# A transformer block on one core: where the MLP phase puts its weight parts, its turned features and its boundary additions

## The chip, the cores and the metric

The kernel runs on one core of a Trainium2 chip. The metric is the device time of one execution in microseconds. A core has five engines, each with a stream of instructions of its own: TensorE (PE in the profile, its weight loads PEld) multiplies matrices into the accumulator memory PSUM, VectorE (DVE), ScalarE (ACT) and GpSimd (POOL) work element by element, and SyncE (SP) issues most DMAs. Engines wait for each other by semaphores only.

## The reference, cut to what matters

One transformer block for 2048 tokens of width D = 640, with a modulation vector made from `c`. First comes an attention half with a linear kernel, which gives A1. The second half is the one in which the change lies:

```python
x = x + ga * A                                   # A1 holds ga * A
h = layernorm(x) * (1 + cb) + sb
r = relu(h @ w1 + b1); r = r * r                 # w1: 640 x 1728
x = x + gb * (r @ w2 + b2)                       # w2: 1728 x 640
```

All is float32. TensorE gets float32 precision from the faster format float32r by splitting each matrix into a high part and a low part and adding three products (high by high, high by low, low by high). So each operand needs a copy that rounds (ScalarE, the high part) and a subtraction (VectorE, the low part).

## The kernel before, in words

The attention half ends about 401 us after the start. The MLP phase, from there to the end, works on blocks of 256 tokens, j = 0 to 7 (`NB` = 8), each held as two tiles i = 0, 1 of 128 tokens. The 1728 columns of w1 are cut into 14 pieces f (13 of 128, the last of 64), taken in pairs n = 0 to 6 (`NP` = 7). So a block is seven steps n, and a step has two half steps, one for each f.

In each half step `up(j, f)` makes the hidden columns (15 matmuls into PSUM tile `up`), ScalarE applies bias and relu (line 1162, `ft<-up`) and VectorE squares (line 1163). After the second half step `split_a` makes high and low part of the squares (`ra`; ScalarE lines 1186 and 1192, VectorE line 88). One step later the products with w2 run as `down(0)` and `down(1)`, one behind each `up`: their stationary operand is `ra`. Blocks 0 and 1 are plain (`PLAIN` = 2): four regions "2", "3", "4", "x" of the result are summed directly. In later blocks most pairs use a scheme with seven products instead of eight, for which sums of hidden columns (`rs`, lines 1177 and 1202) and sums of weights (`ring_a`, `ring_b`, `ring_c`, fetched from DRAM by GpSimd's queue, line 1272, into four buffers) are needed. The accumulators are PSUM banks. Regions 3 and x share one.

Beside these matmuls, the other engines prepare what comes next, and the order in which they do it is written out by hand in the loop of lines 1430 to 1516, for all engines but SyncE. SyncE's DMAs are ordered by the planner, and run as far ahead as their buffers allow.

- **Weight parts.** A part is one of the 28 pieces of w1 and w2. `prep(k)` (line 1377) makes k of them: k copies (`p_hi`, ScalarE line 938), k subtractions (`p_lo`, VectorE line 88, `w<-rw`), and k loads of raw rows for later parts (`p_load`, SyncE lines 928 and 931, `rw<-in_w`). Nine parts are done before the MLP phase. The other 19 are made in block 0: `PREPS` (line 1389) says how many at each of the two calls in a step. `down` and `up` of block 0 need each part a step or more later.
- **LayerNorm of the next block.** `layer(j + 1, at)` (line 1411), with at = 2n or 2n + 1, does what the tables `LN_AT` give for that half step: `load_x1` loads A1 into `xm` and x into two rows `xx`; `add_x` adds them (VectorE line 997) and stores the sum in DRAM (line 998); `ln_pieces` gives six ScalarE pieces, two sums (line 1396) and two squares (line 1401), which write their unused full-size output into the rows `xx`, and two scalings (line 1408), with small work on GpSimd; `t2` turns the normalised tokens: TensorE transposes (line 359, `tb`), ScalarE scales into a buffer `hf` (line 370), ScalarE rounds it (line 371, `h<-hfb`), VectorE subtracts (line 88, `h<-hfb`). `hf` is one buffer of 256 columns in the pool `p3`.
- **The end of a block.** At n = 0 of the next block `first_combos` adds some regions, and `end` adds region by region into the rows `y` (VectorE line 1327; for blocks 0 and 1 line 1330 multiplies by the gate instead), `gate` multiplies by gb, `finish` adds the residual and stores. The residual rows `xr` are loaded from the stored sums (`residual`, line 1317), and `add_bias` (line 1319) adds gb * b2 to them.

Rows of 640 columns come from sets of buffers: `s1` has five, `s2` two. A row asked for from a set waits until the row that last used the slot has been read for the last time. `row("s1", ...)` is used for raw weights, residuals, and the rows `xx` from block 3 on. The w1 weights of f = 13 live in one row of s1 to the end. `s2` holds `y`, the rows `xx` of blocks 1 and 2, and the raw rows of the two parts f = 13 (64 wide).

Of the kernel before, what the change touches and what calls it, by code (L numbers as in the profile page):

```python
# [51 lines left out]
def kernel(  # L52
# [64 lines left out]
    def row(tag, name):  # L117
        return (pc if tag in ("s3", "s4") else mem).tile([P, D], F32, tag=tag, name=name, bufs=BUFS[tag])
# [793 lines left out]
    def prep_load(k, f, w):  # L912
        n = FS[f]
        W = W1 if k == "1" else W2
        if k == "1":
            w = w.rearrange("p s (k n) -> p s k n", k=NC)
        W[f] = w
        i = preps.index((k, f))
        if EARLY_ROWS <= i < EARLY_ROWS + 4:
            if i % 2 == EARLY_ROWS % 2:  # L920
                RAWT.append(tok2(f"w{W_AT[(-19, -16)[len(RAWT)]]}", f"rawt{i}"))
            raw = RAWT[-1][:, (i - EARLY_ROWS) % 2]
        else:
            raw = row("s2" if n < P else "s1", f"rw{k}_{f}")
        if k == "1":
            raw = raw.rearrange("p (k n) -> p k n", k=NC)
        if k == "1":
            nc.sync.dma_start(raw, w1[f * P : (f + 1) * P].rearrange("p (k n) -> p k n", k=NC))
        else:
            for r in range(P // n):  # L930
                nc.sync.dma_start(raw[r * n : r * n + n], w2[f * P : f * P + n])
        RAW[k, f] = raw
# [67 lines left out]
    def t2(j, *ds):  # L1000
        if 0 in ds:
            H2[j] = ht(f"h2_{j}", j, (0, 96))
        if j == 0:
            t_unit(XM[j], cols_b, H2[j], ds[0], f"b{j}", bank(f"tb{j}_{ds[0]}"))
            return
        p = tp(f"tb{j}_{ds[0]}")
        for k, d in enumerate(ds):
            t_in(XM[j], d, p[:, 256 * k : 256 * k + 256])
        for k, d in enumerate(ds):
            hf = p3.tile([P, 256], F32, tag="hf", name=f"hfb{j}_{d}")  # L1010
            t_out(cols_b, H2[j], d, f"b{j}", p[:, 256 * k : 256 * k + 256], hf)

    NB = NT // 2
    places += [new(f"w{w}") for w in W_AT[-23:-19] + W_AT[-18:-16] + W_AT[-15:]] + [new(tag) for tag in ("k", "k", "q0", "q1")]
# [304 lines left out]
    def add_bias(j, i):  # L1319
        add(XR[j, i], XR[j, i], bb)  # L1320
# [56 lines left out]
    def prep(n):  # L1377
        p_hi(n)
        p_lo(n)
        p_load(n)  # L1380
# [5 lines left out]
    LN_AT1 = {"load": 3, "add": (5, 5), "ln": (5, 6, 6, 7, 8, 8), 9: (0, 1), 11: (2, 3), 12: (4,)}  # L1386
    LN_AT2 = {"load": 4, "add": (6, 6), "ln": (7, 7, 8, 8, 9, 9), 10: (0, 1), 11: (2, 3), 12: (4,)}
    LN_AT = {"load": 0, "add": (3, 4), "ln": (4, 5, 6, 6, 7, 7), 8: (0, 1), 10: (2, 3), 12: (4,)}
    PREPS = iter([0, 4] * 5 + [0, 1])

    def ln_pieces(xt, nm, spare):
        sm = small([P, 2], "sm", f"sm{nm}")
# [15 lines left out]
            nc.scalar.activation(xt[:, i], xt[:, i], AF.Identity, bias=nb[:, i : i + 1], scale=sq[:, i : i + 1])  # L1408
            yield

    def layer(j, at):
        todo = {1: LN_AT0, PLAIN: LN_AT1, PLAIN + 1: LN_AT2}.get(j, LN_AT)
        if j == NB:
            return
        if at in todo:
            t2(j, *todo[at])
        if todo["load"] == at:
            load_x1(j)
        for i in range(2):
            if todo["add"][i] == at:  # L1420
                add_x(j, i)
        for i in range(6):
            if todo["ln"][i] == at:
                if i == 0:
                    LN2[j] = ln_pieces(XM[j], f"b{j}", XX[j])
                next(LN2[j])
# [3 lines left out]
    for j in range(NB):  # L1430
        for n in range(NP):
            down = lambda k: prev and (down_plain if plain(*prev) else down_pair)(*prev, k)
            twice = not plain(j, n)
            m = NP * j + n - NP - 1
            done = j - 1 if j and prev else None
            up(j, 2 * n)
            if prev and not plain(*prev):
                split_s(*prev)
            down(0)
            if j < PLAIN:  # L1440
                layer(j + 1, 2 * n)
            if 0 < m < NP - 2:
                t_split(m - 1)
            if m == -1:
                t_load(0)
            if (j, n) == (PLAIN, 0):
                t_fetch(4)
            if j >= PLAIN:
                layer(j + 1, 2 * n)
            prep(next(PREPS, 0))  # L1450
            if n == 0 and j:
                if j - 1 >= PLAIN:
                    first_combos(j - 1)
                else:
                    Y[j - 1] = [row("s2", f"y{j - 1}_{i}") for i in range(2)]
                for r, i, c in (("2", 0, L), ("3", 0, R)):
                    end(j - 1, r, i, c)
            if n == 1 and j:
                gate(j - 1, 0)
                if j != PLAIN:  # L1460
                    finish(j - 1, j < PLAIN)
            if n == 1 and j == PLAIN:
                finish(j - 1, 0)
            if n == 2 and j == PLAIN:
                t_sums(NP - 2)
            if n == (2 if j > PLAIN else 1) and j:
                gate(j - 1, 1)
            if n == (5, 5, 4, 3)[min(j, 3)]:
                residual(j)
            for i in range(2):  # L1470
                if n == 6 and j == 0 or n == 5 and j >= PLAIN and i == 0:
                    add_bias(j, i)
            if j == NB - 1 and n == 1:
                for k in range(NP - LAST, NP - 1):
                    plain_load(k)
            if j == NB - 1 and n == 3:
                for k in range(NP - LAST, NP - 1):
                    plain_split(k)
            if j == NB - 1 and n == NP - 2:
                for i in range(2):  # L1480
                    by_gate(Y[j][i], Y[j][i], slice(0, D))
            if j == NB - 1 and n == NP - 1:
                split_a(j, n, (0,))
                for i in range(2):
                    add(Y[j][i], Y[j][i], XR[j, i])
            up(j, 2 * n + 1)
            if j >= PLAIN and n == 0:
                down(1)
            split_a(j, n, (0, 1) if (j, n) != (NB - 1, NP - 1) else (1,))
            if twice:  # L1490
                sums(j, n)
            if j < PLAIN or n:
                down(1)
            if m == NP + 1:
                t_split(NP - 2)
            prep(next(PREPS, 0))
            if n == 0 and j:
                end(j - 1, "4", 1, L)
                end(j - 1, "x", 1, R)
            if n == (2 if j > PLAIN else 1 if j == PLAIN else 0) and j:  # L1500
                finish(j - 1, j >= PLAIN)
            layer(j + 1, 2 * n + 1)
            if 0 <= m < NP - 2:
                t_sums(m)
            if m == NP - 2:
                t_split(m - 1)
            if 0 < m + 1 < NP - 1:
                t_load(m + 1)
            if m == NP - 1:
                for i in range(2):  # L1510
                    add_bias(j - 1, i)
            if j >= PLAIN and n == 5:
                add_bias(j, 1)
            if j == NB - 1 and n == NP - LAST:
                first_combos(j)
            prev = j, n
# [60 lines left out]
```

## Time and profile before

| | |
|---|---|
| median of 3 runs | 789.05 us (789.01 to 789.47) |
| the profiled execution | 788.85 us |
| span of the profile, first to last instruction | 787.1 us |
| mean granted TensorE clock | 0.998 |
| TensorE busy | 775.0 us, 98% of the span |
| VectorE, ScalarE, GpSimd busy | 583.9, 441.3, 124.3 us |
| share of the DMA engines in use, 401 to 494 / 494 to 547 / 547 to 779 us | about 0.57 / 0.88 / 0.63 |

In the lists of waits a row says which engine and line waited for which, with the total, the number and the longest in microseconds. In a timeline a row gives start, length, engine, line, operation, what is written from what, the shape and how many were merged; a bracket holds the idle time of that engine before the row and what ended it. Line 78 is a helper that issues all matmuls and line 88 one for all low parts, so that the tiles' names tell them apart.

### The profile page before, as it was taken

Reading aid. Unit: us, or ns where it says so; the run is one execution under the profiler, and the core shown is the slowest. Engines: PE = TensorE matmul, PEld = TensorE weight load, DVE = VectorE, ACT = ScalarE, POOL = GpSimd, SP = SyncE. Lnnn points to the kernel's source line nnn. Section 1 sums busy time; section 2 is a strip of 40 time slices with the busy share of each in tenths; the row PEclk is TensorE's granted clock in tenths of the full one; section 3 lists DMA queues with packets and bytes.
Section 4 is the critical chain, followed back from the end, with each engine's and each line's share of the span. In section 5 each row is a group of like instructions: output and inputs, shape, how many; then the busy total and the mean of one; then the engine's idle time right before and its main releaser. Section 6 shows DMA issues by size and latency. Waiting matters only on the chain.

```text
span 787.1 us, 15302 instructions
## 1 busy us (share of the span) xinstructions
PE 775.0 (98%) x5989; PEld 745.6 (95%) x5989; DVE 583.9 (74%) x1059; ACT 441.3 (56%) x988; POOL 124.3 (16%) x253
## 2 busy tenths in 40 slices
PE   9999999999999999999999999999999999999997
PEld 8899999999999889998999999999999999999997
DVE  6599899998788699986256666775757567585756
ACT  5766675475752365656766636455454645536331
POOL 3001101001000232320000001131131313213110
PEclk9999999999999999999999999999999999999999
DMA  9714244432120254222266365897675858657450
GB/s 336 281 59 139 83 152 156 134 113 89 68 102 1 83 169 168 84 100 85 101 194 209 101 208 207 289 319 229 177 221 167 266 149 264 204 169 211 117 168 34
DMA packets 50551, 126.03 MB, mean 160 GB/s; under 512 B 5991, under 2 KB 6759, under 8 KB 50479
## 3 DMA queue, kind: packets, MB, share of 16 engines
q1 hardware_dynamic: 33144, 83.99, 31.1%
q0 software_dynamic: 14752, 35.76, 16.3%
q10 hardware_dynamic: 2583, 5.30, 1.7%
q8 instruction: 47, 0.77, 0.4%
q14 instruction: 25, 0.20, 0.1%
HBM read 95.05 MB, written 29.88 MB: 159 GB/s over the span
## 4 chain that ended last, share of the span: by engine, by line
PE 82%; DVE 5%; DMA 5%; ACT 4%; issue 3%; POOL 1%; POOLq 0%; SPq 0%; ACTq 0%; DVEq 0%
PE up L78 19%; PE acc L78 14%; PE pwo L78 10%; PE pk L78 9%; PE pq L78 8%; PE pv L78 8%; PE acc3x L78 4%; PE kvp L440 3%; PE te L850 2%; DMA ring_b<-td_b 1%; PE numa L78 1%; DMA wm<-in_w_ss 1%; PE tb L359 1%; PE numc L78 1%; PE numb L78 1%
## 5 line engine op out<-in xcount | busy, mean ns | idle before, releaser
L78 PE MATMUL up<-h,w 128*128 128x256 f32 x1640 | 207.1, 278 | 0.4 <-ACT ft L1162 0.4
L78 PEld LDWEIGHTS up<-h,w 128*128 128x128 f32 x1640 | 196.3, 188 | 0.8 <-ACT ft L1162 0.6
L1162 ACT ACTIVATE ft<-up,b_t 128x256 f32<-128x256 f32 x104 | 48.8, 469 | 104.0 <-PE up L78 103.5
L78 PE MATMUL acc<-w,ra 128*128 128x384 f32 x452 | 100.1, 338 | 1.0 <-ACT ra L1186 1.0
L78 PE MATMUL pwo<-wo,ot 128*128 128x256 f32 (+3 forms) x512 | 81.1, 311 | 0.0
L1163 DVE TENSOR_TENSOR ft<-ft 128x256 f32<-128x256 f32 x104 | 44.0, 423 | 48.9 <-ACT ft L1162 47.2
L78 PE MATMUL pk<-wk,hT 128*128 128x384 f32 (+1 forms) x480 | 77.7, 312 | 0.2 <-ACT hT L371 0.2
L78 PEld LDWEIGHTS pwo<-wo,ot 128*128 128x128 f32 (+1 forms) x512 | 74.9, 188 | 2.7 <-issue 2.7
L78 PEld LDWEIGHTS acc<-w,ra 128*128 128x128 f32 x452 | 72.6, 188 | 4.1 <-DVE ra L88 2.8
L78 PE MATMUL pv<-wv,hT 128*128 128x384 f32 (+1 forms) x480 | 76.0, 309 | 0.0
L78 PE MATMUL pq<-wq,hT 128*128 128x384 f32 (+1 forms) x480 | 74.5, 311 | 0.4 <-ACT k L416 0.4
L78 PEld LDWEIGHTS pk<-wk,hT 128*128 128x128 f32 x480 | 71.8, 188 | 2.0 <-ACT hT L371 0.8
L78 PEld LDWEIGHTS pq<-wq,hT 128*128 128x128 f32 x480 | 70.6, 188 | 1.4 <-ACT k L416 0.9
L78 PEld LDWEIGHTS pv<-wv,hT 128*128 128x128 f32 x480 | 70.7, 188 | 0.4
L88 DVE TENSOR_TENSOR ra<-ft,ra 128x384 fp32r<-128x384 f32 (+2 forms) x86 | 36.8, 448 | 34.2 <-ACT ra L1186 21.5
L1186 ACT ACTIVATE ra<-ft 128x384 fp32r<-128x384 f32 x48 | 25.2, 525 | 32.6 <-DVE ft L1163 25.2
L88 DVE TENSOR_TENSOR h<-hfb,h 128x256 fp32r<-128x256 f32 x40 | 17.0, 425 | 35.1 <-ACT h L371 35.1
L78 PE MATMUL acc3x<-w,ra 128*128 128x256 f32 x248 | 43.0, 281 | 0.0
L78 PEld LDWEIGHTS acc3x<-w,ra 128*128 128x128 f32 x248 | 39.5, 188 | 1.6 <-DVE y L1327 1.4
L1272 POOL DMA_DIRECT2D ring_a<-td_a x34 | 18.3, 538 | 128.1 <-PE acc L78 107.4
L1177 DVE TENSOR_TENSOR ft<-ft 128x128 f32<-128x128 f32 x136 | 33.3, 286 | 1.2
L370 ACT ACTIVATE hfb<-tb,cols_b 128x256 f32<-128x256 f32 x40 | 22.5, 562 | 18.9 <-PE tb L359 11.3
(251 smaller groups left out, 1407.7 us busy)
## 6 DMA issues: line engine op xcount, KB each, us to landing
ring_c<-td_c POOLq DMA_DIRECT2D x34, 384.0 KB, 4.5
ring_a<-td_a POOLq DMA_DIRECT2D x34, 384.0 KB, 4.1
ring_b<-td_b POOLq DMA_DIRECT2D x34, 256.0 KB, 4.0
esp<-eq SPq DMA_DIRECT2D x12, 640.0 KB, 2.9
el<-esp SPq DMA_DIRECT2D x12, 640.0 KB, 3.9
rw<-in_w SPq DMA_DIRECT2D x23, 320.0 KB, 4.5
wm<-in_w_mod SPq DMA_DIRECT2D x20, 320.0 KB, 4.3
xb<-in_x SPq DMA_DIRECT2D x8, 640.0 KB, 4.0
```

The source lines that it names most:

```text
L78: nc.tensor.matmul(o, a, b, start=first and i == 0, stop=last and i == len(terms) - 1, skip_group_check=skip,)
L88: (eng or nc.vector).tensor_tensor(out_lo, full, hi.bitcast(F32), op=ALU.subtract)
L359: nc.tensor.transpose(p[:, i * P : (i + 1) * P], xn[:, i, d * P : (d + 1) * P], ident)
L370: nc.scalar.activation(hf, p[:, :256], AF.Identity, bias=cols[:, d : d + 1], scale=cols[:, 5 + d : 6 + d])
L440: nc.tensor.matmul(kvp[g // 4][64 * c : 64 * c + 64, a : a + 2 * n].rearrange("p (s n) -> p s n", s=2), v[:, u], e[:, :, o : o + n], start ...
L850: nc.tensor.transpose(p[:m, a : a + P], EU[2 * j + i][:, b : b + m], ident)
L1162: nc.scalar.activation(r, p, AF.Relu, bias=b1_t[:, f : f + 1])
L1163: nc.vector.tensor_tensor(r, r, r, op=ALU.mult)
L1177: nc.vector.tensor_tensor(t[:, o], t[:, a], t[:, b], op=op)
L1186: nc.scalar.activation(a[:, 0, :3], t[:, :3], AF.Copy)
L1272: nc.gpsimd.dma_start(RING[j, n, r], TD[n][r].bitcast(F32R))
```

## The change

Six edits, all in the MLP phase:

1. The raw rows of the parts f = 13 are taken from s1, like all others, not from s2.
2. `t2` has no buffer `hf` of its own: it uses the first 256 columns of the two rows `xx` in turn, by d % 2. The rows stay in use until the last unit is turned (at = 12).
3. `PREPS`: before, no part in the first half step and four in the second, for five steps, and one at the end. After, two and two for three steps, two and one for two steps, and one at n = 5.
4. In the first half steps of block 0 `layer` is split: turning, loading and adding go ahead of the weight parts, the LayerNorm pieces behind them.
5. In blocks 2 to 7 the bias additions of both tiles stand at n = 5 ahead of `layer`. Before, the first stood behind it and the second at the end of the second half step.
6. At the boundary of two blocks region 3 is ended before region 2.

```diff
@@ -921,7 +921,7 @@ prep_load
-            raw = row("s2" if n < P else "s1", f"rw{k}_{f}")
+            raw = row("s1", f"rw{k}_{f}")
@@ -1007,8 +1007,7 @@ t2
         for k, d in enumerate(ds):
-            hf = p3.tile([P, 256], F32, tag="hf", name=f"hfb{j}_{d}")
-            t_out(cols_b, H2[j], d, f"b{j}", p[:, 256 * k : 256 * k + 256], hf)
+            t_out(cols_b, H2[j], d, f"b{j}", p[:, 256 * k : 256 * k + 256], XX[j][d % 2][:, :256])
@@ -1386,7 +1385,7 @@
-    PREPS = iter([0, 4] * 5 + [0, 1])
+    PREPS = iter([2, 2] * 3 + [2, 1] * 2 + [1])
@@ -1408,17 +1407,20 @@
-    def layer(j, at):
+    def layer(j, at, part=None):
         todo = {1: LN_AT0, PLAIN: LN_AT1, PLAIN + 1: LN_AT2}.get(j, LN_AT)
         if j == NB:
             return
-        if at in todo:
-            t2(j, *todo[at])
-        if todo["load"] == at:
-            load_x1(j)
-        for i in range(2):
-            if todo["add"][i] == at:
-                add_x(j, i)
+        if part != 1:
+            if at in todo:
+                t2(j, *todo[at])
+            if todo["load"] == at:
+                load_x1(j)
+            for i in range(2):
+                if todo["add"][i] == at:
+                    add_x(j, i)
+        if part == 0:
+            return
         for i in range(6):
             if todo["ln"][i] == at:
                 if i == 0:
@@ -1438,7 +1440,7 @@
             if j < PLAIN:
-                layer(j + 1, 2 * n)
+                layer(j + 1, 2 * n, None if j else 0)
@@ -1446,14 +1448,19 @@
             if j >= PLAIN:
+                if n == 5:
+                    for i in range(2):
+                        add_bias(j, i)
                 layer(j + 1, 2 * n)
             prep(next(PREPS, 0))
+            if j == 0:
+                layer(j + 1, 2 * n, 1)
             if n == 0 and j:
...
-                for r, i, c in (("2", 0, L), ("3", 0, R)):
+                for r, i, c in (("3", 0, R), ("2", 0, L)):
                     end(j - 1, r, i, c)
@@ -1468,7 +1475,7 @@
             for i in range(2):
-                if n == 6 and j == 0 or n == 5 and j >= PLAIN and i == 0:
+                if n == 6 and j == 0:
                     add_bias(j, i)
@@ -1509,8 +1516,6 @@
-            if j >= PLAIN and n == 5:
-                add_bias(j, 1)
             if j == NB - 1 and n == NP - LAST:
                 first_combos(j)
```

## The prediction

> **What bounds the kernel now.** I read the page first, then the waits of the weight loads on TensorE over the MLP phase (400 to 788 us), then the timelines around each wait. First the page, then those waits (columns: total us, times, longest).
>
> ```profile
> span 787.1 us, 15302 instructions
> ...
> PE 775.0 (98%) x5989; PEld 745.6 (95%) x5989; DVE 583.9 (74%) x1059; ACT 441.3 (56%) x988; POOL 124.3 (16%) x253
> ```
>
> ```profile
> PEld acc L78 <- DVE ra L88: 2.8, 10, 0.3
> PEld acc L78 <- DMA ring_b<-td_b: 1.8, 1, 1.8
> PEld acc3x L78 <- DVE y L1327: 1.4, 5, 0.3
> PEld acc L78 <- ACT ra L1186: 1.2, 1, 1.2
> PEld up L78 <- ACT ft L1162: 0.6, 1, 0.6
> PEld tb L359 <- ACT hfb L370: 0.4, 1, 0.4
> PEld acc L78 <- DVE rs L88: 0.3, 1, 0.3
> ```
>
> TensorE is the bound, and the change neither adds nor removes a matmul. So it can gain at most these eight or nine microseconds, and can lose only by new waits. The question is which of these rows each edit reaches. The profiled execution took 788.85 us for a span of 787.1 (1.75 lie around it), 0.20 under the median of 789.05; my sum is made from 788.85, and the 0.20 is added at the end.
>
> **Part 1: weight parts two per half step (block 0).** A weight part is one ScalarE copy, one VectorE subtraction and one load. Before, four come together in each second half step. TensorE, then ScalarE, VectorE and SyncE at that place:
>
> ```profile
> 413.29 1.03 PE L78 MATMUL acc<-w,ra 128*128 128x384 f32 x3
> ...
> 418.80 1.86 PE L78 MATMUL up<-h,w 128*128 128x256 f32 x15
> ...
> 422.58 1.86 PE L78 MATMUL up<-h,w 128*128 128x256 f32 x15
> ...
> 429.42 1.86 PE L78 MATMUL up<-h,w 128*128 128x256 f32 x15
> ...
> 432.84 2.03 PE L78 MATMUL up<-h,w 128*128 128x256 f32 x15
> 435.83 1.03 PE L78 MATMUL acc<-w,ra 128*128 128x384 f32 x3 [0.96 <-ACT ra L1186]
> ...
> 437.95 0.60 PE L359 MATMUL tb<-ident,xm 128*128 128x128 f32 x4
> ```
>
> ```profile
> 402.84 0.47 ACT L1162 ACTIVATE ft<-up,b_t 128x256 f32<-128x256 f32 x1 [0.79 <-PE up L78]
> ...
> 406.14 2.61 ACT L938 ACTIVATE w<-rw 128x640 fp32r<-128x640 f32 x4
> ...
> 411.02 0.74 ACT L1396 ACTIVATE xx<-xm 128x640 f32<-128x640 f32 x1 [1.92 <-DVE xm L997]
> ...
> 430.43 2.00 ACT L938 ACTIVATE w<-rw 128x640 fp32r<-128x640 f32 x3 [3.08 <-DMA rw<-in_w]
> 432.33 0.45 ACT L1162 ACTIVATE ft<-up,b_t 128x256 f32<-128x256 f32 x1
> ```
>
> ```profile
> 405.05 0.43 DVE L1163 TENSOR_TENSOR ft<-ft 128x256 f32<-128x256 f32 x1 [1.27 <-ACT ft L1162]
> ...
> 406.89 3.03 DVE L88 TENSOR_TENSOR w<-rw,w 128x640 fp32r<-128x640 f32 x4
> ```
>
> ```profile
> 406.86 0.33 SPq L993 DMA_DIRECT2D xx<-in_x  x1
> ...
> 424.35 0.33 SPq L928 DMA_DIRECT2D rw<-in_w  x1
> ```
>
> Undisturbed, a half step of block 0 takes 432.84 - 429.42 = 3.42 us. From 418.80 to 422.58 it is 3.78, so 0.36 is lost; from 432.84 to 437.95 it is 5.11, so 1.69 is lost. The first kind has a chain: four subtractions (3.03) hold VectorE, the addition of x waits behind them, the LayerNorm piece waits for that with ScalarE idle (1.92), the next activation stands behind the piece, and ra is late. With two parts ahead of the piece and the addition of x ahead of both, that chain is shorter by about two subtractions, 2 x 0.74 (a step, (3.03 - 0.82)/3 with an assumed 0.82 for the last). Gain 0.36 at 420.5. The group at 413.29 has the same length as the one at 435.83, 1.03, and is a twin of this wait (0.36). I give it nothing: there the first newly loaded part may meet its own load. Its bounds are +0.36, if that load goes out at once, and -0.1, if it goes out behind the x row at 406.86 and lands 4.9 us (the median below) after about 407.3.
>
> The 1.69 goes as a whole. The load at 424.35 took a row of the two-buffer set s2, and had to wait until LayerNorm had finished with the x row in it; ScalarE then sat 3.08 us in front of three parts, with the activation at 432.33 behind them. With all raw rows in s1 and the loads spread out, that row's place is free when an earlier subtraction ends, a half step before. One slot of s1 is kept for good by the last W1 weights, so four remain; each part is still loaded at least two half steps (6.8 us) before its copy.
>
> The price: at n = 0 there were no parts ahead of the second activation, now there are two. Their copies take (2.61 - 0.72)/3 = 0.63 each from 403.3 on and end by 404.6, in time for that activation. Their subtractions start at about 404.0 and hold VectorE for 0.74 + 0.74, so the square that began at 405.05 begins at about 405.5. TensorE waits for its result at 406.09 already (one of the ten waits on ra). Loss 0.4, between 0.2 and 0.6.
>
> Block 0: -0.4 + 0.36 + 1.69 = 1.65.
>
> **Part 2: two buffers for turned features.** The buffer hf goes from one buffer to the two x rows, which LayerNorm has finished with. ScalarE waited for the single buffer at every second unit (first row); the second row is block 2, where it matters, and the third is a bias addition that Part 3 moves:
>
> ```profile
> ACT hfb L370 <- DVE h L88: 7.6, 15, 1.0
> ```
>
> ```profile
> 543.24 0.46 ACT L1162 ACTIVATE ft<-up,b_t 128x256 f32<-128x256 f32 x1
> ```
>
> ```profile
> 538.71 0.82 DVE L1327 TENSOR_TENSOR xr<-xr,bb 128x640 f32<-128x640 f32 x1
> ```
>
> Most of the 7.6 us is off the path, since of TensorE's waits only two rows, 1.0 in all, name ft or hfb. It is on the path in block 2, at n = 6, where the waits on ft (0.6), hfb (0.4) and rs (0.3) of the second fence stand, together 1.3. There the bias addition at 538.71 delays a square by 0.74 (a step), the buffer costs 0.5 at each of two units (7.6/15) and more where VectorE is behind, and the activation at 543.24 is late. With both edits it starts when its matmuls end, by my estimate two microseconds sooner. Gain 1.3, bounds 0.7 (the addition alone still in the way) and 1.3. In block 1 two of the ten ra waits and the start of block 2 shift by 0.5; gain 0.4, bounds 0 and 0.9.
>
> The cost of this part is a longer hold: x rows are let go after the last turn (n = 6) instead of after the squares (n = 3). From block 3 on two x rows and two residual rows are then alive in four slots. They fit, but the load of the next x rows moves from mid-block to the block's end. It is hidden as long as it lands before the addition; see the rivals.
>
> **Part 3: both bias additions ahead of the turn at n = 5.** Blocks 3 to 6 each have this (VectorE, then TensorE; the row at 581.68 is the same group without a wait):
>
> ```profile
> 586.83 0.82 DVE L1327 TENSOR_TENSOR xr<-xr,bb 128x640 f32<-128x640 f32 x1
> ```
>
> ```profile
> 581.68 1.20 PE L78 MATMUL acc<-w,ra 128*128 128x384 f32 x6
> ...
> 588.71 1.44 PE L78 MATMUL acc<-w,ra 128*128 128x384 f32 x6
> ```
>
> The addition at 586.83 stands ahead of a square; ra is late by 1.44 - 1.20 = 0.24. Moved ahead of the turn, the two additions (2 x 0.82) fall where VectorE waits for ScalarE's first turned unit. That unit's subtraction is then about 0.2 to 0.4 late, with nothing behind it that TensorE needs at once. Gain 4 x 0.24 = 0.96, bounds 0 and 1.0. In block 7 nothing is turned, and the square has over 0.5 us to spare: 0.
>
> **Part 4: region 3 before region 2 at the boundary.** Blocks 3 to 7 each wait once (1.4 in total) for VectorE to read region 3, whose bank TensorE wants next for region x:
>
> ```profile
> 598.50 0.41 DVE L1327 TENSOR_TENSOR y<-y,acc3x 128x256 f32<-128x256 f32 x1
> ```
>
> ```profile
> 598.32 0.68 PE L78 MATMUL acc<-w,ra 128*128 128x384 f32 x3
> 598.97 0.62 PE L78 MATMUL acc3x<-w,ra 128*128 128x256 f32 x3
> ```
>
> The read ends at 598.91 and TensorE starts at 598.97, though its turn would be 598.32 + 0.52. Region 2's read is 0.47 long in step; put behind, it frees region 3 that much sooner, more than the wait. Region 2's bank is wanted only a half step later. Gain 5 x 0.25 = 1.2, bounds 0 (if the wait were for both reads) and 1.4.
>
> Raw rows of f = 13 in s1 are counted in Part 1. The wait for ring_b (1.8) isn't touched: it is a transfer among stores whose issue moves with TensorE.
>
> **Sum.** 1.65 + 0.4 + 1.3 + 0.96 + 1.2 = 5.5 us. 788.85 - 5.5 + 0.2 = 783.5 us.
>
> **The rivals.**
>
> *The ring wait takes it back.* If the ring_b transfer is bound by the transfers ahead of it, and not by its issue, it lands when it did, and TensorE, 2.1 us earlier after blocks 0 and 1 (1.65 + 0.4), waits 2.1 longer. For it: it took the longest of its kind.
>
> ```profile
> DMA to landing us min/median/max: 2.8/4.0/8.4
> ```
>
> Against it: what is ahead of it is issued by instructions that move too. Time 785.6. The other way round, with less in flight the wait could shrink by its 1.8: 781.7.
>
> *A late part holds up ScalarE.* The engine takes its instructions in order, as the 3.08 us idle shows. If the load of the first new part goes out behind the x row at 406.86 and takes the longest seen in the MLP phase, it lands at about 413.3:
>
> ```profile
> DMA to landing us min/median/max: 2.7/4.9/6.0
> ```
>
> Then copy, LayerNorm piece, activation and square follow, and a copy into ra of about the same length (0.63 + 0.74 + 0.47 + 0.43 + 0.5 = 2.8), 416.1 against the 413.7 (413.29 + 0.4) when TensorE wants it: 2.4 lost, 785.9. The Trainium skill speaks for this one ("TensorE: Matmul & The Clock Gate", Architectural detail): ScalarE and VectorE are strict FIFOs, so LayerNorm put behind a part also waits for that part's load. The trace agrees that nothing overtakes (3.08 us); by that rule alone, with every load at the slow end, the time would be the 785.9.
>
> *Slower: x rows behind the store.* The loads of x rows now wait for the turn. If SyncE's order puts them behind the finished block's second store instead of ahead of the first, they land after VectorE wants them.
>
> ```profile
> 558.97 0.34 SPq L1324 DMA_DIRECT2D out<-y  x1
> ...
> 569.00 0.34 SPq L1324 DMA_DIRECT2D out<-y  x1
> ```
>
> ```profile
> 561.60 0.82 DVE L997 TENSOR_TENSOR xm<-xm,xx 128x640 f32<-128x640 f32 x1
> ```
>
> Behind the first store a row lands near 564.7 (0.8 for the issue, the 4.9 above to land); the addition is 3.1 late and TensorE, by an estimate, half of that, four times 1.5: no change, 789.5. Behind the second it lands near 574.7, 13 late, some 11 of them TensorE's, four times: about 828. It decides from a landing some 4 us after 561.60. Against it: the rows are free for loading from about 545, sixteen microseconds ahead.
>
> *Nothing comes of it.* Each wait might be replaced by the next one ending just behind: 789.0. Against it: for the largest (1.69) the engine behind it had 3.08 us of idle to give.
>
> **How the numbers follow.** What this kernel's runs can tell is about 0.2%, 1.6 us. Forecast 0.60 (its own range 782.2 to 784.8, by the bounds of the parts), ring wait kept 0.13, ring wait gone 0.05, late part 0.08: all faster, 0.86. Nothing comes of it 0.05: same. X rows behind the store 0.09: slower. The range from 781.5 to 787.0 holds the faster cases with some unknown cost, and leaves out the last two.
>
> **What would show it.** Part 1: no ScalarE idle on rw near 430, and no half step over 3.6 us in block 0 but the first, where ra should be some 0.4 later. Part 2: the row of ScalarE waiting for hfb is gone, and block 2's n = 6 has no wait on ft. Part 3: ra groups at n = 5 at 1.20. Part 4: no wait of acc3x on y. Wrong would be: a new ScalarE wait for rw at 408 to 413, VectorE idle before L997, or ring_b waiting over 3 us.

## The result, and the profile after

The changed kernel takes 784.1 us, the median of six executions (782.46 to 786.04), against 788.98 for the kernel before beside it (787.63 to 789.47). The ratio is 0.9937, with a 95% interval of 0.9923 to 0.9950: faster by 4.9 us at the medians; the same code, compared twice more below, came out 6.1 and 6.8 faster. Forecast were 783.5 us and a range of 781.5 to 787.0. The profiled execution took 782.46 us, the shortest of the six, so that between the two profiled executions 6.4 us went. The page of the changed kernel, then the waits of its weight loads over the MLP phase:

```profile
span 780.8 us, 15291 instructions
...
PE 769.9 (99%) x5989; PEld 745.0 (95%) x5989; DVE 585.1 (75%) x1059; ACT 440.0 (56%) x988; POOL 124.8 (16%) x253
```

```profile
PEld acc L78 <- DMA ring_b<-td_b: 1.3, 1, 1.3
PEld acc L78 <- DVE ra L88: 0.5, 2, 0.3
PEld acc L78 <- ACT ra L1185: 0.5, 1, 0.5
PEld acc L78 <- issue: 0.2, 1, 0.2
PEld acc3x L78 <- DVE ra L88: 0.2, 1, 0.2
```

Of the 8.7 us of before (the seven rows of the prediction's list and one of 0.2 that equals the last row here), 2.7 are left, and half of that is the ring. The waits on y, ft, hfb and rs are gone; of the ten on VectorE's ra two are left. (Line numbers after 1010 are lower by one in the changed kernel.)

Where the time went is read from the length of each block, from the start of its first up group on TensorE to that of the next block (block 7: to the end), in us, one profiled execution each. The second last column is the idle time of TensorE that its own rows in block 2 put down to ring_a and ring_b. The last is the median of all executions less that of the kernel before run beside it; the kernels named here are those of the experiments below. One of the single buffer's nine executions took 1281 us at a mean granted clock of 0.557 and is left out of its median.

| kernel | block 0 | 1 | 2 | 3 | 4 to 6, each | 7 | ring | median |
|---|---|---|---|---|---|---|---|---|
| before | 47.99 | 48.54 | 49.36 | 46.67 | 46.5 | 54.15 | 1.6 | |
| changed | 45.99 | 48.25 | 47.69 | 45.92 | 45.9 | 53.89 | 1.1 | -4.9 |
| end order alone | 46.87 | 48.55 | 49.77 | 46.23 | 46.2 | 53.91 | 1.6 | -1.1 |
| bias alone | 47.99 | 48.54 | 48.34 | 46.44 | 46.5 | 54.13 | 1.0 | -1.2 |
| s1 rows alone | 46.48 | 48.55 | 50.30 | 46.53 | 46.5 | 54.15 | 1.3 | -1.8 |
| first part alone | 47.71 | 48.53 | 51.88 | 46.63 | 46.5 | 54.17 | 2.5 | -0.1 |
| changed, again | 47.36 | 48.26 | 47.70 | 45.92 | 45.9 | 53.91 | 1.4 | -6.1 |
| changed, a third time | 47.08 | 48.22 | 47.99 | 45.92 | 45.9 | 53.91 | 1.4 | -6.8 |
| changed, parts in bursts | 46.48 | 48.26 | 47.84 | 45.92 | 45.9 | 53.90 | 1.5 | -6.3 |
| changed, single buffer | 46.01 | 48.56 | 48.89 | 46.13 | 46.1 | 53.91 | 1.5 | -2.1 |
| changed, old bias places | 45.99 | 48.24 | 50.66 | 45.92 | 45.9 | 53.90 | 2.5 | -4.8 |
| changed, LayerNorm first | 48.85 | 48.24 | 47.75 | 45.92 | 45.9 | 53.92 | 1.4 | -3.6 |
| changed, late parts | 45.54 | 48.24 | 50.93 | 46.19 | 45.9 | 53.92 | 2.5 | -7.5 |
| late parts, late residual | 45.55 | 48.24 | 45.99 | 45.92 | 45.9 | 53.55 | 0 | -8.4 |

Before against changed: 2.00 + 0.29 + 1.67 + 0.75 + 3 x 0.59 + 0.26 = 6.7, less 0.35 by which block 0 started later, is the 6.4 of the two executions. Two columns vary between executions of one and the same code: block 0 (before and bias alone 47.99, end order alone 46.87, though none of these edits touches it) and block 2. Block 3 varies by up to 0.3, and the 53.55 of the last row differs from the others only behind the last matmul. The other columns repeat to some 0.05.

### The profile page after: what moved, and what is told of

Same layout as the page of the kernel before. It is cut to its first block, busy times and chain, and to the rows that moved or that the text cites. A ratio compares the mean times of both kernels' runs of the same rounds, so it can differ in the third digit from the quotient of the medians.

```text
span 780.8 us, 15291 instructions
## 1 busy us (share of the span) xinstructions
PE 769.9 (99%) x5989; PEld 745.0 (95%) x5989; DVE 585.1 (75%) x1059; ACT 440.0 (56%) x988; POOL 124.8 (16%) x253
## 4 chain that ended last, share of the span: by engine, by line
PE 90%; DMA 3%; DVE 3%; ACT 2%; issue 1%; POOL 0%; POOLq 0%; ACTq 0%
PE up L78 23%; PE acc L78 17%; PE pwo L78 10%; PE pk L78 9%; PE pq L78 8%; PE pv L78 8%; PE acc3x L78 5%; PE kvp L440 3%; PE te L850 2%; PE tb L359 1%; PE numa L78 1%; DMA wm<-in_w_ss 1%; DMA ring_b<-td_b 1%; DMA xb<-in_x 1%; PE numc L78 1%
## 5 line engine op out<-in xcount | busy, mean ns | idle before, releaser
L78 PE MATMUL acc<-w,ra 128*128 128x384 f32 x452 | 97.8, 335 | 0.3 <-ACT ra L1185 0.3
L88 DVE TENSOR_TENSOR h<-xx,h 128x256 fp32r<-128x256 f32 x35 | 14.9, 425 | 21.9 <-ACT h L371 21.9
L468 DVE TENSOR_REDUCE rs_q<-eq 128x64 f32<-128x1280 f32 x16 | 23.6, 1479 | 10.0 <-ACT eq L427 10.0
```

The lines of the kernel that those rows point to most:

```text
L78: nc.tensor.matmul(o, a, b, start=first and i == 0, stop=last and i == len(terms) - 1, skip_group_check=skip,)
L88: (eng or nc.vector).tensor_tensor(out_lo, full, hi.bitcast(F32), op=ALU.subtract)
L468: nc.vector.tensor_reduce(s, heads(flat(e)), axis=AX.X, op=ALU.add)
```

## The experiments

### Each small edit alone

**End order alone.** The kernel before, with region 3 read first:

```diff
-                for r, i, c in (("2", 0, L), ("3", 0, R)):
+                for r, i, c in (("3", 0, R), ("2", 0, L)):
```

> The kernel before with only the end order changed (region 3 read before region 2). Own-wait theory: each of the five waits of acc3x on y (1.4 us in all) goes and nothing takes its place: 1.2 us less than before (1.0 to 1.4), the waits on ra, rw, hfb and ring_b as before. Rival, that the wait was for both reads: the row stays or turns into a wait of acc on y of the same size, no change. Rival, that the next wait is right behind it: the row is gone but the blocks are not shorter.

787.81 us against 788.88 (ratio 0.9987, interval 0.9971 to 1.0004). TensorE at the boundary that the prediction showed (there acc3x began 0.65 after acc, at 598.97 after 598.32), now:

```profile
597.26 0.68 PE L78 MATMUL acc<-w,ra 128*128 128x384 f32 x3
597.78 0.51 PE L78 MATMUL acc3x<-w,ra 128*128 128x256 f32 x3
```

acc3x follows after 0.52, its turn. The interval alone would allow no change at all, so the blocks decide: blocks 4 to 6 are 0.26 shorter each. The own-wait theory holds: five times 0.26 is 1.3 (1.1 at the medians), where 1.2 was summed.

**Bias alone.** The kernel before, with both additions ahead of the turn at n = 5:

```diff
             if j >= PLAIN:
+                if n == 5:
+                    for i in range(2):
+                        add_bias(j, i)
                 layer(j + 1, 2 * n)
...
-                if n == 6 and j == 0 or n == 5 and j >= PLAIN and i == 0:
+                if n == 6 and j == 0:
...
-            if j >= PLAIN and n == 5:
-                add_bias(j, 1)
```

> The kernel before with only the bias additions moved ahead of the turn at n = 5. Own-wait theory: in blocks 3 to 6 four waits on ra of 0.24 to 0.34 go (1.0 to 1.3), and of block 2's 1.3 at n = 6 some 0.6 goes, since the addition at 538.71 no longer delays a square: 1.3 to 1.9 less than before. Shared-cause theory, by which the single buffer hf is what makes block 2 late: block 2 stays as long as before and only the 1.0 to 1.3 goes. Rival: the additions hold up the subtraction of the first turned unit, a new wait of TensorE on h, no gain.

787.71 against 788.88 (0.9986, 0.9972 to 1.0000). But the gain isn't where either theory had most of it: blocks 3 to 6 are shorter by 0.23, -0.07, 0.06 and -0.12, 0.1 together; the 1.0 is in block 2, nearly all at n = 6. VectorE, then ScalarE in block 4 at n = 5:

```profile
628.03 1.56 DVE L1327 TENSOR_TENSOR xr<-xr,bb 128x640 f32<-128x640 f32 x2
629.50 0.42 DVE L88 TENSOR_TENSOR h<-hfb,h 128x256 fp32r<-128x256 f32 x1
```

```profile
629.96 0.56 ACT L370 ACTIVATE hfb<-tb,cols_b 128x256 f32<-128x256 f32 x1 [0.62 <-DVE h L88]
630.56 0.42 ACT L371 ACTIVATE h<-hfb 128x256 fp32r<-128x256 f32 x1
630.88 0.46 ACT L1162 ACTIVATE ft<-up,b_t 128x256 f32<-128x256 f32 x1
```

The additions hold up the subtraction of the first turned unit; with one buffer ScalarE's second unit waits for that subtraction (0.62), and the activation at 630.88 stands behind it. The wait on ra at n = 5 went, and others of about 0.1 came.

**Two buffers taken out, or the bias put back.** From the changed kernel, once with the single buffer hf again (the raw rows stay in s1), once with the bias additions in their old places:

```diff
-            t_out(cols_b, H2[j], d, f"b{j}", p[:, 256 * k : 256 * k + 256], XX[j][d % 2][:, :256])
+            hf = p3.tile([P, 256], F32, tag="hf", name=f"hfb{j}_{d}")
+            t_out(cols_b, H2[j], d, f"b{j}", p[:, 256 * k : 256 * k + 256], hf)
```

> The changed kernel with the single buffer hf again; the s1 rows, the spread, the bias additions and the end order stay. Enabling theory (the single buffer holds ScalarE's second turned unit behind VectorE, and takes back what the bias additions give): blocks 3 to 6 take 46.2 instead of 45.91, as with the end order alone (46.24), block 2 0.5 to 1.0 more and block 1 0.3 more: 1.9 to 2.5 slower than the changed kernel. Independent theory, as predicted: blocks 3 to 6 stay at 45.91, block 1 loses 0.3 and block 2 0.6: 1.0 slower.

> The changed kernel with the bias additions in their old places. Independent theory, as predicted: a wait on ra of 0.24 returns at n = 5 in each of blocks 3 to 6: 1.0 slower. Enabling theory: with two buffers ScalarE and VectorE are about 1.4 us ahead there and an addition takes 0.74, so nothing returns: blocks 3 to 6 at 45.9 to 46.0, 0 to 0.3 slower in all.

On the same chip, before 788.14: single buffer 786.0 (ratio 0.9972, 0.9957 to 0.9987), old bias places 783.4 (0.9943, 0.9923 to 0.9963). With the single buffer blocks 3 to 6 are 0.21 longer each, block 1 0.31, and block 2 0.8 besides the ring (1.2 in all, less 0.4 of ring). Of block 2's part about 0.5 lies at n = 0, 5 and 6; another 0.5 lies at n = 2 and 3, where the end-order and the late-part run, one of them with two buffers, lost 0.3 to 0.4 too, so that it can't be put down to the buffer. ScalarE, then TensorE, in block 4 of the single-buffer run:

```profile
629.37 0.56 ACT L370 ACTIVATE hfb<-tb,cols_b 128x256 f32<-128x256 f32 x1 [0.63 <-DVE h L88]
629.97 0.42 ACT L371 ACTIVATE h<-hfb 128x256 fp32r<-128x256 f32 x1
630.29 0.46 ACT L1162 ACTIVATE ft<-up,b_t 128x256 f32<-128x256 f32 x1
```

```profile
630.39 0.50 PE L78 MATMUL acc<-ring_b,rs 128*128 128x256 f32 x3
630.80 1.99 PE L78 MATMUL up<-h,w 128*128 128x256 f32 x15
```

The up group starts 0.05 after the late activation (630.29 + 0.46 = 630.75) has read its bank, 0.41 instead of 0.34 after ring_b, and is 0.13 longer. With two buffers and the additions in their old places nothing of that is left, nor the old wait on ra. VectorE and TensorE of that run:

```profile
630.02 0.82 DVE L1326 TENSOR_TENSOR xr<-xr,bb 128x640 f32<-128x640 f32 x1
630.75 0.42 DVE L1162 TENSOR_TENSOR ft<-ft 128x256 f32<-128x256 f32 x1
631.76 0.56 DVE L88 TENSOR_TENSOR ra<-ft,ra 128x384 fp32r<-128x384 f32 x1 [0.59 <-ACT ra L1185]
```

```profile
630.78 1.86 PE L78 MATMUL up<-h,w 128*128 128x256 f32 x15
632.49 1.20 PE L78 MATMUL acc<-w,ra 128*128 128x384 f32 x6
```

The addition still stands ahead of the square, but ra is done at 632.3, before TensorE wants it. So the enabling theory holds: the two buffers give what was put down to the bias additions. These, moved, are worth 0.1 in blocks 3 to 6 without the buffers and nothing with them. In block 2 at n = 6 each edit alone gives most of it: the step takes 7.6 us before, 6.7 with the bias alone, 6.6 with the single buffer, and 6.4 both in the changed kernel and with the old bias places. (The rest of block 2 in the old-bias run, 50.66, is the ring and the clock, which the late-part run, with the additions moved, shows too.)

### The first part and the first new weight part

**S1 rows alone, and the whole first part alone.** The kernel before, with the one line, and then with the spread and the divided layer step too:

```diff
-            raw = row("s2" if n < P else "s1", f"rw{k}_{f}")
+            raw = row("s1", f"rw{k}_{f}")
...
-    PREPS = iter([0, 4] * 5 + [0, 1])
+    PREPS = iter([2, 2] * 3 + [2, 1] * 2 + [1])
```

> The kernel before with only the raw rows of f = 13 put in s1. Row theory: the load at 424.35 was late because of the s2 row alone; ScalarE's 3.08 us idle near 430 goes and with it the whole 1.69 of TensorE; the 0.36 to 0.39 lost in each burst of four parts stays: 1.7 less than before (1.5 to 1.8). Burst theory: the load comes late because four parts come together, and stays late in s1: ScalarE still waits over 1 us there, under 0.7 gained. Ring theory: TensorE is 1.7 earlier from block 0 on, and the wait for ring_b at block 2 grows from 1.8 to about 3.4: no change in all.

> The kernel before with the whole of the first part: two weight parts per half step, LayerNorm behind them, raw rows in s1. Theory: block 0 is 2.0 us shorter, as with the whole change (-0.44 at the first ra, +0.39 and +0.35 at the two bursts, +1.69 at the s2 row), so that beside the run with the s1 rows alone the spread gives only 0.3: 1.9 to 2.1 less than before. Ring theory: the wait for ring_b grows by those 2.0 and the time is that of before. Rival, that the spread is worth nothing without the other parts: the same time as with the s1 rows alone.

S1 rows: 787.09 against 788.88 (0.9977, 0.9966 to 0.9988), block 0 1.51 shorter, and ScalarE no longer waits for a load there; the row theory holds. The whole first part: 788.76 (0.9990, 0.9979 to 1.0000), no faster than the s1 rows alone, rather slower. Its ScalarE and TensorE in block 0:

```profile
407.60 0.73 ACT L938 ACTIVATE w<-rw 128x640 fp32r<-128x640 f32 x1
411.53 0.74 ACT L938 ACTIVATE w<-rw 128x640 fp32r<-128x640 f32 x1 [3.19 <-DMA rw<-in_w]
```

```profile
414.41 1.04 PE L78 MATMUL acc<-w,ra 128*128 128x384 f32 x3 [1.11 <-ACT ra L1186]
```

ScalarE waits 3.19 us for the first newly loaded part, the LayerNorm piece and the next activation stand behind it, and TensorE waits for ra. Block 0 is 1.7 longer for it than with the whole change (47.71 and 45.99, the same order of parts). None of the three theories had that.

**The changed kernel again, and three variants of its parts.** "Parts in bursts" is the changed kernel with the PREPS of before and an undivided layer step. "Late parts" has none in the first half step:

```diff
-    PREPS = iter([2, 2] * 3 + [2, 1] * 2 + [1])
+    PREPS = iter([0, 2] + [2, 2] * 3 + [2, 1, 2])
```

"Part load first" calls the first two parts ahead of the layer step at n = 0:

```diff
+            if n == 0 and j == 0:
+                prep(next(PREPS, 0))
             if j < PLAIN:
                 layer(j + 1, 2 * n, None if j else 0)
```

> The changed kernel once more, as the control for the three beside it. Late-part theory (the first newly loaded part lands between 0 and 2 us too late, by the execution, and costs TensorE 0 to 1.3): a median of 784 with executions from 782.4 to 786, and where the profiled one is slow, ScalarE waits over 2 us for rw near 410 and TensorE for ra near 414. Ring theory: the spread is the ring_b wait alone, 1.3 in the profile at 782.46 and some 3 us in a slow one.

> The changed kernel with the parts in bursts of four again, as before; the s1 rows, the x rows as buffers, the bias additions and the end order stay. By the sum of the single waits the spread is worth 0.39 + 0.35 - 0.44 = 0.3: 0.3 slower than the changed kernel. Late-part theory: the spread brings the wait for the first new part, so that without it the time is as much lower as the run with the whole first part was above the run with the s1 rows alone, 1.7 at the medians: 782.4. Rival, that the first part's missing gain was in block 2 (the clock and the ring of that one run): the same as the changed kernel within 0.4.

> The changed kernel with no parts in the first half step and two in each from the second on. Late-part theory: the first load goes out about where it did, behind the x row, but its part is copied a half step (3.4 us) later, so ScalarE no longer waits for it; and the two subtractions no longer delay the first square: 0.44 less than the changed kernel for the square, and 0 to 1.3 for the part, a median 0.6 to 1.5 lower, with less spread. Rival, that the parts at the far end get late: a wait for w or rw near 430 to 440, no gain.

> The changed kernel with the first two parts and the loads behind them ahead of the load of the x row on SyncE's queue at n = 0; ScalarE's and VectorE's order is not changed. Late-part theory, that the queue makes the load late: it goes out about 1.5 us sooner (near 405), ScalarE's wait for rw at 408 to 411 is under 0.3 in every execution, the first square is as late as before (0.44): 0 to 1.2 below the changed kernel. Transfer theory, that the load is slow in its transfer and not in its issue: ScalarE's wait is as long, no gain. Rival: the x row, now behind, is late for its addition, and VectorE waits at L997.

Before 789.1; again 783.0 (0.9914, 0.9885 to 0.9944); bursts 782.8 (0.9919, 0.9892 to 0.9946); late parts 781.6 (0.9901, 0.9869 to 0.9933); part load first 782.3 (0.9924, 0.9896 to 0.9952). These intervals overlap, so here the traces decide. Late parts lie 1.4 below "again" at the medians, as their first theory had it, but not with less spread (3.9 against 2.8 us). In the three executions of the changed kernel the rings took 1.1, 1.4 and 1.4 us, not some 3, so the ring theory of its spread is not borne out in these. The order of SyncE's queue is not written out by hand in this phase, and with "part load first" every engine's instructions came out in the order of the changed kernel: that run tests no load, and is the table's third execution of the changed kernel. ScalarE's wait for the first new part, in the first, second and third:

```profile
410.50 0.74 ACT L938 ACTIVATE w<-rw 128x640 fp32r<-128x640 f32 x1 [1.28 <-DMA rw<-in_w]
```

```profile
412.22 0.74 ACT L938 ACTIVATE w<-rw 128x640 fp32r<-128x640 f32 x1 [2.84 <-DMA rw<-in_w]
```

```profile
411.81 0.74 ACT L938 ACTIVATE w<-rw 128x640 fp32r<-128x640 f32 x1 [2.68 <-DMA rw<-in_w]
```

Against the first, block 0 is 1.4 longer in the second and 1.1 in the third, and 1.7 behind the 3.19 above: TensorE loses what goes beyond some 1.5 us. Its wait in the second execution:

```profile
415.11 1.04 PE L78 MATMUL acc<-w,ra 128*128 128x384 f32 x3 [0.75 <-ACT ra L1185]
```

The load goes out at the same place each time (SyncE's queue of the changed kernel, first, and again, second):

```profile
407.17 0.38 SPq L928 DMA_DIRECT2D rw<-in_w  x1
```

```profile
407.46 0.38 SPq L928 DMA_DIRECT2D rw<-in_w  x1
```

So it is the landing that varies, from 3.3 (410.50 - 407.17) to 4.8 us (412.22 - 407.46) after the issue; why it does is not shown. With late parts that wait is 0.23, none comes later, and the first group waits less (TensorE of late parts, then of the changed kernel):

```profile
405.83 1.04 PE L78 MATMUL acc<-w,ra 128*128 128x384 f32 x3
```

```profile
406.83 1.04 PE L78 MATMUL acc<-w,ra 128*128 128x384 f32 x3 [0.28 <-ACT ra L1185]
```

Block 0 is then 45.5, the shortest of all. With bursts it is 46.5, between the changed kernel at its best (46.0) and at its worst (47.4). The spread is thus worth 0.5 when the first part lands early and costs 0.9 when it lands late; by the medians it is worth nothing (783.0 and 782.8). Why the first part alone came out 1.7 above the s1 rows alone at the medians, when with the rest the spread costs nothing, is not settled: its profile shows 1.7 at the part and a slowed clock in block 2 (below), but how many of its eleven executions had these no run shows.

**LayerNorm first.** The changed kernel with the layer step undivided ahead of the parts:

```diff
-                layer(j + 1, 2 * n, None if j else 0)
+                layer(j + 1, 2 * n)
...
-            if j == 0:
-                layer(j + 1, 2 * n, 1)
```

> The changed kernel with the LayerNorm pieces of block 0 ahead of the weight parts instead of behind them. Theory that this order matters: the piece waits for the addition of x, the parts and the next activation wait behind the piece, and TensorE waits for ra at n = 1 and 2, about 0.36 each as before: 0.4 to 0.8 slower. Theory that only the bursts matter: two parts leave room for either order, block 0 as long as with the changed kernel (46.0 to 47.4 by the first part's landing), no difference.

784.54 against 788.14 (0.9950, 0.9933 to 0.9968), 1.2 above the run with the old bias places on the same chip. ScalarE and TensorE:

```profile
409.70 0.74 ACT L1395 ACTIVATE xx<-xm 128x640 f32<-128x640 f32 x1 [1.71 <-DVE xm L997]
410.44 0.72 ACT L938 ACTIVATE w<-rw 128x640 fp32r<-128x640 f32 x1
412.49 0.74 ACT L938 ACTIVATE w<-rw 128x640 fp32r<-128x640 f32 x1 [1.34 <-DMA rw<-in_w]
```

```profile
415.04 1.04 PE L78 MATMUL acc<-w,ra 128*128 128x384 f32 x3 [1.43 <-ACT ra L1185]
```

The piece waits 1.71 for the addition of x with both copies behind it, and then the load takes another 1.34: block 0 is 48.85, 1.5 longer than the changed kernel with a late part and 2.9 longer than with an early one. Of the 2.9, 2.0 are lost in this half step, and 0.9 in two later ones. The order matters, as the first theory had it; its 0.4 to 0.8 fits the two later half steps, and the load, which it left out, came on top in the first.

### The ring, and a kernel below both

In block 2 the late-part run and two others were longer than the table's pattern allows. Late parts, TensorE (its last group runs on beyond the view), and then single microseconds of the same run (us busy and instructions of PE, PEld, DVE, ACT and POOL, then the granted TensorE clock, the DMA engines' share and GB/s):

```profile
526.34 0.76 PE L78 MATMUL acc<-ring_a,rs 128*128 128x384 f32 x3 [0.68 <-DMA ring_a<-td_a]
...
529.59 0.99 PE L78 MATMUL acc<-ring_b,rs 128*128 128x256 f32 x3 [1.79 <-DMA ring_b<-td_b]
530.38 2.90 PE L78 MATMUL up<-h,w 128*128 128x256 f32 x13
```

```profile
527.00:528.00 1.00, 0.80 (x7) 0.60 (x5) 0.78 (x3) 0.19 (x1) 0.48 (x1) 1.00 1.16 380
528.00:529.00 1.00, 0.00 (x0) 0.00 (x0) 0.68 (x3) 0.10 (x1) 0.15 (x1) 1.00 0.84 284
529.00:530.00 1.00, 0.41 (x2) 0.41 (x3) 0.00 (x0) 0.82 (x1) 0.00 (x0) 0.82 0.82 264
530.00:531.00 1.00, 1.00 (x6) 1.00 (x6) 0.00 (x0) 0.54 (x1) 0.01 (x1) 0.50 0.26 81
...
532.00:533.00 1.00, 1.00 (x7) 1.00 (x6) 0.00 (x0) 0.00 (x0) 0.00 (x0) 0.50 0.80 162
533.00:534.00 1.00, 1.00 (x8) 1.00 (x8) 0.00 (x0) 0.45 (x2) 0.00 (x0) 0.97 0.68 234
```

Here TensorE waited for ring_a and ring_b one after the other, and then ran at half clock for some 3.4 us (from about 529.6 to 533.0). Half of that, about 1.7 us, is lost on top of the waits. The old-bias run and the first part alone show the same, with 0.50 for 3.4 us from 529.7 and 531.4. Waits of up to 1.64, as in the kernel before and with the end order alone, left the clock at 1.00.

From 515 to 530 us the DMA engines have hardly any free time. In the changed kernel their share is 0.96 to 1.14 in each three microseconds, of which the first and the last (same columns):

```profile
515.00:518.00 3.00, 3.00 (x24) 3.00 (x23) 2.97 (x10) 2.37 (x6) 0.54 (x1) 1.00 1.03 300
...
527.00:530.00 3.00, 1.88 (x16) 1.68 (x15) 1.83 (x6) 1.45 (x2) 1.04 (x2) 1.00 1.14 399
```

In that burst stand two loads of residual rows, whose addition can wait (SyncE's queue of the changed kernel):

```profile
518.79 1.68 SPq L1316 DMA_DIRECT2D xr<-x  x2
```

**Late residual** is the late-part kernel with these two loads, in block 2 alone, a half step or two later on GpSimd's queue, whose order is written out:

```diff
-            nc.sync.dma_start(t, X1[j][:, i])
+            (nc.gpsimd if j == PLAIN else nc.sync).dma_start(t, X1[j][:, i])
...
-                if n == 5:
+                if n == 5 + (j == PLAIN):
...
-            if n == (5, 5, 4, 3)[min(j, 3)]:
+            if n == (5, 5, 5, 3)[min(j, 3)]:
```

> The kernel with the late parts (none in the first half step), and in block 2 alone the two loads of residual rows a half step or two later, on GpSimd's queue, with their bias additions at n = 6. Burst theory (from 515 to 530 us all 16 DMA engines are busy and ring_b waits its turn): 0.66 MB less in front of ring_b, 1.8 us at the 364 to 399 GB/s of that stretch, so the waits for ring_a and ring_b of 0.8 + 2.0 shrink to under 0.7 together and the clock stays at 1.00 behind them: 1.3 to 2.5 less than with the late parts alone at the medians of comparable executions, near 780.0. Chain theory (ring_b waits only for the store of its own data and the tile before it): the wait stays at 1.3 to 2.0. Rival: the loads on GpSimd's queue hold up the ring fetches behind them, a new wait at n = 5 or 6.

779.71 against 788.14 (778.83 to 780.30; ratio 0.9891, 0.9874 to 0.9909). Its interval ends under that of the changed kernel's first comparison (0.9923) but overlaps those of the two later ones, which begin at 0.9885 and 0.9896. All four executions lie below all eighteen of that code, of which the shortest took 781.29, though the kernel before was 1.0 faster beside them than beside that one. Against late parts it is 1.9 lower as measured and 0.9 when each is taken against the kernel before beside it; 1.3 to 2.5 was expected. Its waits over the MLP phase, and the transfers from 515 to 533 us (KB each, median us to landing), first of late parts, then of this kernel:

```profile
PEld acc L78 <- DVE ra L88: 0.5, 2, 0.3
PEld acc3x L78 <- DVE ra L88: 0.2, 1, 0.2
```

```profile
ring_a<-td_a POOLq DMA_DIRECT2D x2, 384.0 KB, 7.9
```

```profile
ring_a<-td_a POOLq DMA_DIRECT2D x3, 384.0 KB, 4.0
```

No wait on a ring is left, block 2 is as long as blocks 3 to 6, and the tiles land sooner. The burst theory holds in this execution, the shortest of the four; two loads fewer were enough. The loads went out later and on another queue at once, so which of the two counted is not shown. Four executions are few, but they lie within 1.5 us, where those of late parts span 3.9.

## Why the prediction was right

The time lies 0.6 from the forecast, and the sum of 5.5 between the 4.9 of the medians and the 6.4 of the profiled executions. That the two are so close is in part luck: by the blocks the change is worth 6.7 when the first new part lands early, more than the sum, and a late landing, which the sum left out, takes 1.1 to 1.4 of it back. And two steps had the wrong reason, and one chance was far off.

**Part 1.** The raw rows were right: ScalarE's idle time on rw near 430 is gone, and so is the 1.69. That number was one execution's, though. In the end-order run, whose block 0 is the code of before, block 0 is 1.1 shorter; so the gain lies between about 0.6 and 1.7 by the execution. The price at the first ra was 0.44 (0.4 forecast), and the wait at 420.5 gave 0.35 (0.36). What failed is the step "I give it nothing ... bounds are +0.36 ... and -0.1" for the twin at 413.29: it gave 0.39 in the first profiled execution and cost 0.9 and 0.7 in the next two (half steps of 4.72 and 4.50 against 3.81 before). The lower bound placed the landing about right (407.3 + 4.9 = 412.2; measured 412.2 in the second execution), but then did not add what stands behind it. The prediction's own sign of being wrong here, a ScalarE wait for rw at 408 to 413, stood in all three profiles of the changed kernel (1.28, 2.84 and 2.68).

**The rival of the late part** did add it: landing plus 2.8 us for copy, LayerNorm piece, activation, square and copy. For a landing at 412.2 that gives 415.0, and TensorE started at 415.11. Its mechanism was right; its size, 2.4, was taken from the longest landing (413.3), where 1.1 to 1.7 was measured. Its chance of 0.08 was wrong: of six profiled executions with this order of parts (three of the changed kernel; first part alone, single buffer, old bias places) three lost time so. It turned no sign, since the rest gave more. The strict order of ScalarE that the Trainium skill states ("TensorE: Matmul & The Clock Gate", Architectural detail) agrees with the 2.84 us in front of one part while the piece and the activation stood behind.

**Parts 2 and 3.** Together 2.7 were summed (0.4 + 1.3 + 0.96), and the blocks show about that: 0.29 in block 1, 1.67 in block 2 (1.2 of it at n = 6, where 1.3 was forecast, and most of the rest ring), and 0.3 in each of blocks 3 to 6 beside the end order. ScalarE's 7.6 us of waiting for the single buffer are gone. But the split was wrong. The step that failed is "That unit's subtraction is then about 0.2 to 0.4 late, with nothing behind it that TensorE needs at once": with one buffer the second turned unit and the next activation are behind it, as the bias-alone run shows. And "on the path in block 2" was too narrow for the buffer: it is on the path wherever VectorE is late at a turn, and TensorE's waits didn't name it because the addition stood later in the chain and came last. Taken out, the buffers cost 1.6 to 2.3 by the blocks (0.31 + 0.5 to 1.2 + 4 x 0.21), and the bias move nothing. In block 2 the two edits reach the same delay, so that there, too, their gains can't be summed.

**Part 4** is right in place and size: 1.2 forecast, 1.3 by the blocks and 1.1 by the medians of the run that has it alone.

**The ring and the slower rival.** The wait for ring_b was said to be untouched. It was 1.3 instead of 1.8, and over fourteen profiled executions TensorE's idle time for the rings runs from 0 to 2.5, and doesn't follow how early TensorE is: from block 0's start to block 2's the changed kernel took 94.2 us and had 1.1, the run with the old bias places took 94.2 and had 2.5. So neither form of the ring rival is borne out as a rule; a third, two waits and the clock behind them, was not foreseen. The rows for the slower rival, SyncE's queue and VectorE of the changed kernel at the start of block 3:

```profile
539.48 0.33 SPq L993 DMA_DIRECT2D xx<-in_x  x1
542.68 0.40 SPq L993 DMA_DIRECT2D xx<-in_x  x1
555.07 0.34 SPq L1323 DMA_DIRECT2D out<-y  x1
```

```profile
557.57 0.81 DVE L997 TENSOR_TENSOR xm<-xm,xx 128x640 f32<-128x640 f32 x1
```

Both x rows go out ahead of the first store, twelve microseconds before it, and the addition waits for nothing.

## What to carry to other kernels

A wait that names only the last instruction of a chain hides the ones behind it: before two edits are given their own sums, ask whether the one only moves the work in front of the other's wait, and try them apart. A stall on a transfer seen in one execution is one draw: read it in several executions, and give a first load, which has no steady distance yet, one half step more rather than an average landing. Where the DMA engines are full ahead of a wait, look for a transfer in the burst that nobody needs yet; moving two such loads left none of the 1.1 to 2.5 us of waits in the execution profiled here.

## What the runs showed that was not expected

Two waits of TensorE in quick succession, 0.68 and 1.79, 1.34 and 1.19, or 1.49 and 0.99 us, each pair within some 4 us, came with a granted clock of 0.50 for about 3.4 us, from near the end of the second wait on, in each of the three executions that had them, a loss of about 1.7 beyond the waits. Waits of 1.0 to 1.64 in all, one or two of them, as in the other executions with the ring's old burst, were not. The Trainium skill ("TensorE: Matmul & The Clock Gate", HAM oscillation) puts the rule as "no PE-idle gaps >~3.4µs"; here no gap was longer than 1.8, and the clock halved nonetheless. Each pair sums to about 2.5 and no single wait went beyond 1.8, so whether their sum, their number or their place in time decides is not shown.
